# Turning v on VectorE instead of TensorE in a channel-attention and rational-FFN kernel, and adding sums of squares by accumulating DMA

## The chip, the core and the metric

The kernel runs on one core of a Trainium2 chip. The metric is the device time of one execution in microseconds (us): 2692.88 as the median of three runs, from 2692.05 to 2693.2. TensorE does the matrix products, VectorE, ScalarE and GpSimd the elementwise work, and SyncE issues the plain DMAs. In the rows these are PE (PEld is PE's weight load), DVE, ACT, POOL and SP.

## The reference

```python
# per batch b of 4: q, k, v are [6080, 256]
qn = q / (norm(q, axis=1) + 1e-6)        # norm of each column over the 6080 rows
kn = k / (norm(k, axis=1) + 1e-6)
s = kn.T @ qn / tau                      # [256, 256] for each batch
a = exp(s - s.max(-1)); a /= a.sum(-1) + 1e-9
x = (v @ a).reshape(24320, 256)
h = x @ w_in                             # [24320, 2048]
P = a0 + a1*h + a2*h**2 + a3*h**3
Q = 1 + |b0|*|h| + |b1|*h**2
out = (P / (Q + 1e-6)) @ w_out           # [24320, 256]
```

w_in and w_out are float64; everything else is float32.

## The kernel before, in words

The two products `v @ a` and `x @ w_in` are fused: for each batch the kernel forms `a @ w_in` once (`fuse`, eight pieces, split into a high and a low part `whi`, `wlo`), and then multiplies v by it. Precision is kept by such splits: v, too, is split into `vhi` and `vlo`.

Rows go in groups of 512 tokens (the last group of a batch has 448), 12 to a batch, 48 in all. For a group, `values` (line 740) loads v into `vst`, turns it so that its 256 columns lie on the partitions (eight TensorE transposes into a PSUM slot), copies the turned slot to `vhi` on ScalarE, and subtracts on VectorE to get `vlo`. Then eight calls of `pair` (line 766) each take 256 of the 2048 hidden columns: two times six matmuls give h in a PSUM slot `hx` (three slots of two banks), ScalarE, VectorE and GpSimd work out the rational function on tiles of 128x1024 or on halves of 128x512, and `mm2` multiplies by `w_out` into the PSUM tile `acc`. Four of the eight pairs (kind R) split their result into `gh` and `gl` for fast products; the other four (kind S) give one tile `g`, multiplied in full float32, for which the trace has two matmul records each. `finish` (line 884) copies `acc` to SBUF, turns it back on TensorE, copies it again and stores it.

Beside this runs the next batch's attention (`Attn.half`, line 538): 24 half tiles of k and q are loaded, multiplied (`products`), squared on ScalarE into one of two `sq` buffers, and added up on GpSimd into `ssq` for the norms. For batch 0 all of it stands before the first group, and its adds are shared by GpSimd and VectorE. Two batches take their 24 halves within some three groups shortly before they are needed; I call these groups those with score products, and the others, which do nothing but eight pairs and the two turnings, plain groups.

The order is found before anything is issued. Each piece of work is a `step` with an engine, a cost, a due time (`key`, from the tables LAG and TIME) and the buffers that it reads and writes. `Planner.order` runs these through a list scheduler: an engine that is free takes the ready step with the lowest key whose buffers fit the counts in SLOTS. The instructions are then issued in that order, and each engine runs its own in order, with semaphores between engines. So a wait on one instruction holds up everything behind it on that engine.

Of the kernel before, what the change touches and what calls it, by code (L numbers as in the profile page):

```python
# [20 lines left out]
LAG = {  # L21
    "first": (-23.943, 0.779, 16.152, -2.628, 12.275, -14.299, 0.849, 12.204),
    "second": (64.578, 55.323, 59.143, 56.607, 7.413, 49.338, 52.686, 69.362),
    "line": (11.809, -44.33, -0.798, -23.493, 7.232, -28.691, -20.654, -32.78),
    "prod": (-25.799, -25.066, -7.177, -0.027, 1.503, -30.754, -29.951, -14.021),
    "abs": (22.851, -16.828, -6.381, 4.349, 3.845, 0.375, -1.748, -5.521),
    "slope": (-2.413, -14.175, 23.292, -11.592, 10.064, 22.358, 14.327, 33.823),
    "num1": (102.929, 82.894, 81.158, 62.614, 64.142, 120.209, 89.073, 104.516),
    "num2": (-4.828, -66.826, -23.076, -34.364, -51.549, -56.374, -41.833, -65.959),
    "sum": (4.693, 16.192, 3.118, 9.167, 1.798, 5.734, -2.218, 21.491),  # L30
    "root": (8.815, 1.931, -7.534, -8.44, 11.521, 1.596, -18.294, 11.215),
    "one": (27.21, 31.412, 40.487, 22.316, 24.471, -12.593, 43.293, 5.876),
    "square": (-64.503, -49.599, -58.591, -28.542, -47.268, -42.996, -32.677, -8.585),
    "quot": (40.746, 32.008, 16.16, 51.527, 29.306, 35.7, 39.709, 24.527),
    "again": (-61.355, -87.995, -84.935, -58.616, -91.448, -79.4, -44.502, -69.519),
    "rest": (-17.013, -33.435, -9.224, -61.671, -10.183, -41.213, -23.935, -25.063),
    "last": (-39.442, -40.174, -68.15, -83.691, -21.902, -24.741, -46.676, -44.956),
    "last_pool": (-0.493, -59.623, -7.515, -32.037, 18.764, -45.886, -12.678, -10.454),
    "out": (63.96, 25.995, 31.164, 31.971, 24.821, 19.268, 27.921, 33.051),
    "out_lo": (116.352, 93.718, 68.074, 61.654, 91.315, 121.222, 76.822, 102.449),  # L40
}
TIME = {
    "pair": 6.5, "start": 92.588, "load": 1.191, "softmax": 58.031, "in": 2.437,
    "late_in": -22.444, "out0": -54.096, "out": 7.105, "attn0_0": 31.018, "attn_0": 1.206,
    "attn0": 69.854, "attn": 0.995, "attn1": 94.156, "value": 1.073, "fuse": 5.271,
    "finish": -40.738, "front": 35.456, "front_pace": 13.309, "back": 50.586, "store": 55.554,
    "ahead_pe": 283.994, "ahead_act": 1891641.487, "ahead_dve": 6393007968.0, "ahead_pool": 11581445.34,
# [3 lines left out]
KIND = ("RFP", "SU", "RFP", "SF", "RFP", "SU", "RFP", "SF")  # L51
# [59 lines left out]
def flat(bufs):  # L111
    return [x for b in bufs for x in (b.both if isinstance(b, Pair) else [b])]


class Planner:
# [5 lines left out]
    HOP = {"PE": 0.25, "ACT": 0.07, "DVE": 0.07, "POOL": 0.07, "SP": 3.5}  # L121
# [39 lines left out]
    def order(self):  # L161
# [113 lines left out]
def tile_channel_attention_rational_ffn(  # L275
# [41 lines left out]
    def apart(eng, ins):  # L317
# [15 lines left out]
    pool = InOrder(tc, nc.gpsimd, apart)  # L333
# [5 lines left out]
    plan = Planner(SLOTS, ("d", "uu", "r", "gh", "gl", "g", "w", "kq", "sq", "vst", "vhi", "vlo", "orow", "acc"), ("hA", "hB", "acc"),  # L339
# [176 lines left out]
    class Attn:  # L516
# [21 lines left out]
        def half(self, i, at, both, sps):  # L538
# [35 lines left out]
            else:  # L574
# [5 lines left out]
                step(*(("DVE", 1.2) if own else ("POOL", 2.38)), at + 2, fn, [sq, total], [total], True)  # L580
# [389 lines left out]
```

## Time and profile before

| what | us |
|---|---|
| median of three runs | 2692.88 |
| the profiled execution's own time | 2693.56 |
| its span, first to last instruction | 2691.8 |
| TensorE busy | 2601.5 (97%) |
| VectorE busy | 2473.1 (92%) |
| GpSimd busy | 2287.1 (85%) |
| ScalarE busy | 2238.9 (83%) |

The busy time of TensorE counts pipelined matmuls that overlap, so its real pace is read from the starts of neighbours in the timeline. The mean granted TensorE clock over the span is 0.992 of full speed. In the rows below, "x" is a count, and the number behind "|" is busy time in us and the mean of one in ns.

### The profile page before, as it was taken

How to read it: one execution, taken by the hardware profiler on the slowest of the kernel's cores; microseconds unless marked ns; L12 is line 12 of the kernel's file. 1: busy time of each engine (PE TensorE's matmuls, PEld its weight loads, DVE VectorE, ACT ScalarE, POOL GpSimd, SP SyncE). 2: the span in 40 equal slices, each digit the busy share in tenths (PEclk: the TensorE clock that was granted, in tenths of full speed). 3: DMA queues.
4: the chain of work that ended last, by engine and by line, in shares of the span. 5: the costliest groups of instructions: out<-in, count | busy, mean ns of one | idle time of the engine just before them, and what ended most of it. 6: DMA issues, size and time to landing. Idle time of an engine off the chain costs nothing.

```text
span 2691.8 us, 30390 instructions
## 1 busy us (share of the span) xinstructions
PE 2601.5 (97%) x10304; PEld 1864.0 (69%) x10304; DVE 2473.1 (92%) x2911; ACT 2238.9 (83%) x2285; POOL 2287.1 (85%) x1725
## 2 busy tenths in 40 slices
PE   7899999999999999999999999999999999999998
PEld 5766667666766666667777667667777666667666
DVE  8889998899979999998888999999888999999998
ACT  5688887788888888888878888888786888898896
POOL 6598888888768888889978898888996898898897
PEclk9899999999999999999999999999999999999999
DMA  9400002000100000012210000001220000000000
GB/s 318 139 18 16 24 16 85 16 16 31 41 22 16 24 24 16 24 40 77 79 60 15 32 15 17 32 16 47 78 77 24 23 8 24 32 8 24 31 9 15
DMA packets 69324, 109.97 MB, mean 41 GB/s; under 512 B 5296, under 2 KB 53936, under 8 KB 69168
## 3 DMA queue, kind: packets, MB, share of 16 engines
q1 hardware_dynamic: 69168, 108.03, 12.0%
q8 instruction: 81, 1.33, 0.2%
q14 instruction: 75, 0.61, 0.1%
HBM read 83.10 MB, written 24.90 MB: 40 GB/s over the span
## 4 chain that ended last, share of the span: by engine, by line
DVE 38%; PE 33%; POOL 11%; issue 8%; ACT 8%; DMA 1%; SPq 0%; DVEq 0%; POOLq 0%; ACTq 0%
PE hx L64 18%; PE acc L64 15%; DVE hx L64 13%; DVE d L64 9%; DVE uu L64 7%; POOL d L64 7%; DVE g L64 4%; DVE gh L64 3%; ACT uu L64 3%; ACT r L64 2%; POOL gl L64 2%; POOL ssq L64 2%; DVE vlo L64 1%; ACT d L64 1%; POOL orow L64 1%
## 5 line engine op out<-in xcount | busy, mean ns | idle before, releaser
L64 PE MATMUL hx<-vhi,w 128*128 128x512 f32 (+1 forms) x3072 | 1094.5, 413 | 42.4 <-DVE g L64 25.1
L64 PEld LDWEIGHTS hx<-vhi,w 128*128 128x128 f32 x3072 | 578.4, 188 | 240.2 <-DVE g L64 51.8
L64 PE MATMUL acc<-g,w_out_sb 128*128 128x512 f32 (+1 forms) x1536 | 688.9, 587 | 1.1 <-DVE g L64 1.1
L64 POOL TENSOR_TENSOR d<-d,gh 128x512 f32<-128x512 f32 (+1 forms) x384 | 484.2, 1282 | 192.4 <-DVE gh L64 191.9
L64 PE MATMUL hx<-vlo,w 128*128 128x512 f32 (+1 forms) x1536 | 598.5, 390 | 0.0
L64 ACT ACTIVATE uu<-hx,babs 128x1024 f32<-128x1024 f32 (+1 forms) x384 | 423.3, 1102 | 164.9 <-PE hx L64 163.1
L64 POOL TENSOR_TENSOR gl<-d,r 128x512 fp32r<-128x512 f32 (+1 forms) x384 | 489.7, 1283 | 19.9 <-DVE d L64 18.7
L64 DVE SCALAR_TENSOR_TENSOR hx<-uu,coef,hx 128x1024 f32<-128x1024 f32 (+1 forms) x384 | 488.9, 1273 | 3.5
L64 POOL TENSOR_TENSOR d<-d,r 128x512 f32<-128x512 f32 (+1 forms) x384 | 481.3, 1276 | 10.6 <-ACT r L64 8.1
L64 DVE TENSOR_TENSOR uu<-uu,hx 128x1024 f32<-128x1024 f32 (+1 forms) x384 | 461.7, 1202 | 27.8 <-ACT uu L64 27.0
L64 PEld LDWEIGHTS acc<-g,w_out_sb 128*128 128x128 f32 x1536 | 289.9, 189 | 273.1 <-issue 254.7
L64 ACT ACTIVATE uu<-hx,coef 128x1024 f32<-128x1024 f32 (+1 forms) x384 | 457.0, 1190 | 0.0
L64 ACT ACTIVATE r<-d 128x1024 f32<-128x1024 f32 (+1 forms) x384 | 401.9, 1047 | 37.6 <-POOL d L64 34.6
L64 ACT ACTIVATE d<-d 128x1024 f32<-128x1024 f32 (+1 forms) x288 | 301.4, 1047 | 140.7 <-DVE d L64 140.3
L64 ACT ACTIVATE r<-r 128x1024 f32<-128x1024 f32 (+1 forms) x384 | 402.2, 1048 | 5.7
L64 DVE SCALAR_TENSOR_TENSOR d<-uu,babs,hx 128x1024 f32<-128x1024 f32 (+1 forms) x288 | 364.2, 1264 | 29.3 <-ACT uu L64 25.9
L64 POOL TENSOR_SCALAR d<-d,ones 128x1024 f32<-128x1024 f32 (+1 forms) x288 | 322.6, 1120 | 78.0 <-ACT r L64 77.1
L64 PEld LDWEIGHTS hx<-vlo,w 128*128 128x128 f32 x1536 | 290.0, 189 | 72.6 <-issue 26.8
L64 DVE SCALAR_TENSOR_TENSOR d<-hx,coef,d 128x512 f32<-128x512 f32 (+1 forms) x384 | 282.9, 741 | 51.8 <-POOL d L64 51.6
L64 DVE SCALAR_TENSOR_TENSOR hx<-hx,coef,r 128x512 f32<-128x512 f32 (+1 forms) x384 | 288.4, 751 | 22.7 <-ACT r L64 13.4
L64 DVE SCALAR_TENSOR_TENSOR gh<-hx,coef,r 128x512 fp32r<-128x512 f32 (+1 forms) x384 | 269.4, 740 | 23.9 <-ACT r L64 15.4
L64 DVE SCALAR_TENSOR_TENSOR g<-d,hx 128x512 f32<-128x512 f32 (+1 forms) x384 | 257.3, 679 | 20.4 <-POOL d L64 6.5
(101 smaller groups left out, 2990.1 us busy)
## 6 DMA issues: line engine op xcount, KB each, us to landing
vst<-in_v_dram SPq DMA_DIRECT2D x44, 512.0 KB, 3.4
out_dram<-orow SPq DMA_DIRECT2D x44, 512.0 KB, 2.6
kq<-in_k_dram SPq DMA_DIRECT2D x78, 256.0 KB, 3.5
kq<-in_q_dram SPq DMA_DIRECT2D x78, 256.0 KB, 3.8
d<-in_moe_w_in_dram SPq DMA_DIRECT2D x8, 512.0 KB, 6.5
r<-in_k_dram SPq DMA_DIRECT2D x10, 256.0 KB, 6.0
r<-in_q_dram SPq DMA_DIRECT2D x10, 256.0 KB, 6.0
d<-in_moe_w_out_dram SPq DMA_DIRECT2D x4, 512.0 KB, 5.7
```

The lines of the kernel that those rows point to most:

```text
L64: ins = op(*args, **kwargs)
```

## The change

v is loaded in four DMAs that already place 32x32 blocks where they belong, in runs of 32 floats (128 bytes) instead of 4 KB, and one VectorE instruction turns the blocks. The turned v lies in one of the two `orow` buffers in SBUF, which `finish` uses as well, and no longer in a PSUM slot. GpSimd makes `vlo`. The sums of squares of batches 1 to 3 are added by a DMA issued from GpSimd that accumulates into `ssq`; each must wait until the one before has landed. Output rows are stored in four DMAs of 1 KB runs. The S pairs write their result over `y` instead of a buffer `g`, halves of `gh` and `gl` share a tile, there is one buffer less for the fused weights, the planner gets other delays between engines, and LAG and TIME have new numbers throughout. The kinds of pairs and their arithmetic are the same; `OUT` stays on TensorE.

```diff
 LAG = {
-    "again": (-61.355, -87.995, -84.935, -58.616, -91.448, -79.4, -44.502, -69.519),
+    "again": (-142.994, -152.496, -145.689, -152.346, -180.413, -123.122, -130.534, -108.094),
...
-KIND = ("RFP", "SU", "RFP", "SF", "RFP", "SU", "RFP", "SF")
+KIND = ("RFPh", "SUPh", "RFPh", "SFPh", "RFPh", "SUPh", "RFPh", "SFPh")
+OUT = "PE"
+SSQ = "DMA"
+VIN = "DVE"
+VLO = "POOL"
...
-    HOP = {"PE": 0.25, "ACT": 0.07, "DVE": 0.07, "POOL": 0.07, "SP": 3.5}
+    HOP = {"PE": 0.22, "ACT": 0.05, "DVE": 0.05, "POOL": 0.05, "SP": 3.5}
+    POOL_HOP = 0.09
+    SAME = {"PE": 0.0, "ACT": 0.03, "DVE": 0.1, "POOL": 0.05, "SP": 0.0}
...
-    SLOTS = {"hA": 3, "hB": 3, "acc": 1, "d": 3, "uu": 4, "r": 3, "gh": 6, "gl": 4, "g": 4, "w": 9, "kq": 4, "sq": 2, "ssq": 1,
+    SLOTS = {"hA": 3, "hB": 3, "acc": 1, "d": 3, "uu": 5, "r": 3, "gh": 3, "gl": 2, "w": 8, "kq": 4, "sq": 2, "ssq": 1,
...
                 fn = lambda: e.tensor_tensor(total[:pn], sq[:pn], total[:pn], op=ALU.add)
-                step(*(("DVE", 1.2) if own else ("POOL", 2.38)), at + 2, fn, [sq, total], [total], True)
+                if SSQ == "DMA" and not first:
+                    begun = Buf()
+                    fn = lambda: pool.dma_start(total[:pn], sq[:pn], accum_op=ALU.add)
+                    step("POOL", 1.0, at + 2, fn, [sq, total], [begun])
+                    step("SP", 0.1, at + 2, lambda: None, [begun, sq, total], [total])
+                else:
+                    step(*(("DVE", 1.2) if own else ("POOL", 2.38)), at + 2, fn, [sq, total], [total], True)
...
     def values(G, at, gate=()):
         vst = buf("vst", [P, T, C], F32)
-        slot = banks()
-        fn = lambda: sp.dma_start(vst[:pn], v[b, base : base + pn * T].rearrange("(p t) c -> p t c", t=T))
-        step("SP", 1.5, at - 3 * II, fn, gate, [vst])
-        def turned():
-            for c in range(NC2):
-                for t in range(T):
-                    pe.transpose(
-                        slot[:, c, t * pn : (t + 1) * pn], vst[:pn, t, c * P : (c + 1) * P], ident[:pn, :pn]
-                    )
-        step("PE", 1.1, at, turned, [vst], [slot, hi, lo])
-        step("ACT", 1.05, at + 1, lambda: act.activation(hi[:, :, :n], slot[:, :, :n], AF.Copy), [slot], [hi])
-        fn = lambda: dve.tensor_tensor(
-        step("DVE", 1.2, at + 2, fn, [slot, hi], [lo])
+        def load():
+                src = rows.rearrange("(j k) (e q i) -> q j k e i", k=K, q=4, i=32)
+                for x in range(4):
+                    dst = vst[32 * x : 32 * x + 32].rearrange("p t c -> p (t c)")[:, : K * 64]
+                    sp.dma_start(dst.rearrange("p (k e i) -> p k e i", e=NC2, i=32), src[x])
+        step("SP", 2.0, at - 3 * II, load, gate, [vst])
+            turned = buf("orow", [P, NC2, GT], F32, "vT")
+            def turn():
+                dve.transpose(
+                    turned[:, :, :n].rearrange("p e (k j) -> p k e j", j=32),
+                    vst.tile.rearrange("p t c -> p (t c)")[:, : K * 64].rearrange("p (k e i) -> p k e i", e=NC2, i=32),
+                )
+            step("DVE", 1.2, at, turn, [vst], [turned])
+        fn = lambda: act.activation(hi[:, :, :n], turned[:, :, :n], AF.Copy)
+        step("ACT", 1.05, at + 1, fn, [turned], [hi])
+        e, eng, cost = (dve, "DVE", 1.2) if VLO == "DVE" else (pool, "POOL", 2.38)
+        step(eng, cost, at + 2, fn, [turned, hi], [lo])
...
     def finish_pe(G, at, acc):
-        fn = lambda: sp.dma_start(out[row : row + pn * T].rearrange("(p t) e -> p t e", t=T), orow[:pn])
+        dst = out[row : row + n].rearrange("(i k) e -> i k e", k=K)
+        def send():
+            for x in range(4):
+                sp.dma_start(dst[:, x:K:4, :], orow[32 * x : 32 * x + 32, : len(range(x, K, 4))])
```

How the change moves instructions is seen in the order of each engine. First TensorE, near the end of a plain group of batch 1 (`ident` is the identity by which v, `vst`, is turned). Before:

```order
L64 MATMUL acc_92<-gl_146,w_out_hi 128x512 x2
L64 MATMUL acc_92<-g_149,w_out_sb 128x512 x2
L64 MATMUL acc_92<-g_150,w_out_sb 128x512 x2
L64 MATMUL hx_153<-ident,vst_130 128x128 x8
L64 MATMUL hx_151<-vhi_132,w_118 128x512
L64 MATMUL hx_151<-vlo_134,w_118 128x512
```

Now, at the end of the same group:

```order
L68 MATMUL hx_142<-vlo_134,w_121 128x512
L68 MATMUL hx_142<-vhi_132,w_129 128x512
L68 MATMUL acc_94<-gh_138,w_out_hi 128x512 x2
L68 MATMUL acc_94<-gh_138,w_out_lo 128x512 x2
L68 MATMUL hx_144<-vhi_131,w_114 128x512
L68 MATMUL hx_144<-vlo_133,w_114 128x512
```

The turning of v, which stood between the float32 products of one group and the next h in a PSUM slot of its own, is gone, and the next h follows other products.

Next VectorE in the same group, where the low part of v stood. Before:

```order
L64 SCALAR_TENSOR_TENSOR hx_152<-hx_152,coef,r_102 128x512 x2
L64 SCALAR_TENSOR_TENSOR g_147<-d_85,hx_152 128x512
L64 SCALAR_TENSOR_TENSOR g_148<-d_85,hx_152 128x512
L64 TENSOR_TENSOR uu_91<-uu_91,hx_153 128x1024
L64 TENSOR_TENSOR vlo_133<-hx_151,vhi_131 128x1024
L64 SCALAR_TENSOR_TENSOR hx_153<-uu_91,coef,hx_153 128x1024
L64 SCALAR_TENSOR_TENSOR gh_137<-hx_153,coef,r_101 128x512
L64 SCALAR_TENSOR_TENSOR gh_138<-hx_153,coef,r_101 128x512
```

Now:

```order
L68 SCALAR_TENSOR_TENSOR hx_142<-hx_142,coef,r_103 128x512 x2
L68 SCALAR_TENSOR_TENSOR uu_89<-d_87,hx_142 128x512
L68 SCALAR_TENSOR_TENSOR gh_137<-hx_144,coef,r_104 128x512
L68 SCALAR_TENSOR_TENSOR uu_89<-d_87,hx_142 128x512
L68 SCALAR_TENSOR_TENSOR gh_137<-hx_144,coef,r_104 128x512
L68 STREAM_TRANSPOSE orow_100<-vst_130 128x16x2x32
L68 SCALAR_TENSOR_TENSOR d_87<-uu_92,babs,hx_143 128x1024
```

`vlo` gives way to the turning of v; the halves of two pairs (`uu`, which takes the place of `g`, and `gh`) are now interleaved.

Then GpSimd in a group with score products of batch 1. Before:

```order
L64 TENSOR_TENSOR d_87<-d_87,r_103 128x512 x2
L64 TENSOR_TENSOR d_85<-d_85,gh_139 128x512
L64 TENSOR_TENSOR d_85<-d_85,gh_140 128x512
L64 TENSOR_TENSOR ssq_136<-sq_99,ssq_136 128x1024
L64 TENSOR_TENSOR gl_145<-d_85,r_102 128x512
L64 TENSOR_TENSOR gl_146<-d_85,r_102 128x512
L64 TENSOR_SCALAR d_86<-d_86,ones 128x1024
L64 TENSOR_TENSOR ssq_136<-sq_100,ssq_136 128x1024
L64 TENSOR_TENSOR d_86<-d_86,r_101 128x512 x2
```

Now:

```order
L68 TENSOR_TENSOR d_86<-d_86,gh_139 128x512 x2
L68 DMA ssq_136<-sq_102 128x1024
L68 TENSOR_TENSOR gl_141<-d_86,r_104 128x512 x2
L68 TENSOR_SCALAR d_87<-d_87,ones 128x1024
L68 DMA ssq_136<-sq_101 128x1024
L68 TENSOR_TENSOR d_87<-d_87,r_103 128x512 x2
L68 TENSOR_SCALAR d_88<-d_88,ones 128x1024
L68 TENSOR_SCALAR d_86<-d_86,babs 128x1024
L68 DMA ssq_136<-sq_102 128x1024
```

Each add of 128x1024 has become the issue of a DMA, with two or three other instructions between one and the next.

Last, GpSimd at the start, where batch 1's first accumulations stand ahead of the first group (the names in brackets are the semaphores waited for; DMASW0 to DMASW7 are those of the accumulating DMAs in turn):

```order
L68 DMA ssq_136<-sq_102 128x1024 [waits Activation_49]
L68 DMA ssq_136<-sq_101 128x1024 [waits DMASW0_49,Activation_49]
L68 TENSOR_TENSOR vlo_133<-orow_100,vhi_131 128x1024 [waits Activation_49]
L68 DMA ssq_136<-sq_102 128x1024 [waits DMASW1_49,Activation_49]
L68 DMA ssq_136<-sq_101 128x1024 [waits DMASW2_49,Activation_49]
L68 DMA ssq_136<-sq_102 128x1024 [waits DMASW3_49,Activation_49]
L68 DMA ssq_136<-sq_101 128x1024 [waits DMASW4_49,Activation_49]
```

Each accumulation waits for the one before; before the change these were adds, which follow each other on the engine.

## Rows read from the trace of the kernel before

**Rows 1.** The page's first part: busy time, share, instructions by engine.
```profile
PE 2601.5 (97%) x10304; PEld 1864.0 (69%) x10304; DVE 2473.1 (92%) x2911; ACT 2238.9 (83%) x2285; POOL 2287.1 (85%) x1725
```

**Rows 2.** Windows: length, busy us by engine, clock, DMA; plain groups, their sum.
```profile
2124.20:2627.70 503.50, 493.44 (x1921) 343.79 (x1921) 488.33 (x551) 437.16 (x431) 439.57 (x342) 1.00 0.06 20
sum 1511.00, PE 1480.65 PEld 1030.20 DVE 1464.27 ACT 1309.83 POOL 1318.58; mean PE 296.13 PEld 206.04 DVE 292.85 ACT 261.96 POOL 263.72
```

**Rows 3.** Timeline of TensorE: start us, length us, instruction, count.
```profile
1048.19 0.62 PE L64 MATMUL acc<-gh,w_out_hi 128*128 128x512 f32 x2
...
1049.56 3.59 PE L64 MATMUL acc<-g,w_out_sb 128*128 128x512 f32 x8
1052.99 1.04 PE L64 MATMUL hx<-ident,vst 128*128 128x128 f32 x8
1055.14 0.50 PE L64 MATMUL hx<-vhi,w 128*128 128x512 f32 x1 [1.12 <-DVE g L64]
```

**Rows 4.** Timeline of TensorE in a group with score products.
```profile
1310.21 1.04 PE L64 MATMUL acc<-ident,orow 128*128 128x128 f32 x8
1311.09 3.62 PE L64 MATMUL hx<-kq 128*128 128x256 f32 x16
```

**Rows 5.** Waits of TensorE in the plain groups from 1465 to 1818.5.
```profile
PE hx L64 <- DVE g L64: 5.2, 5, 1.2
```

**Rows 6.** Groups by form: count, busy us, mean ns, idle before it, releasers.
```profile
L64 DVE SCALAR_TENSOR_TENSOR hx<-uu,coef,hx 128x1024 f32<-128x1024 f32 x352 | 452.1, 1284 | 3.0
...
L64 DVE TENSOR_TENSOR uu<-uu,hx 128x1024 f32<-128x1024 f32 x352 | 427.1, 1213 | 14.5 <-ACT uu L64 13.7
...
L64 DVE SCALAR_TENSOR_TENSOR d<-uu,babs,hx 128x1024 f32<-128x1024 f32 x264 | 336.8, 1276 | 25.2 <-ACT uu L64 24.3 <-issue 0.8
...
L64 DVE SCALAR_TENSOR_TENSOR hx<-hx,coef,r 128x512 f32<-128x512 f32 x352 | 266.3, 757 | 21.4 <-ACT r L64 13.0 <-ACT uu L64 0.5
L64 DVE SCALAR_TENSOR_TENSOR d<-hx,coef,d 128x512 f32<-128x512 f32 x352 | 261.2, 747 | 46.6 <-POOL d L64 46.5
L64 DVE SCALAR_TENSOR_TENSOR gh<-hx,coef,r 128x512 fp32r<-128x512 f32 x352 | 248.6, 746 | 23.4 <-ACT r L64 15.4
...
L64 DVE SCALAR_TENSOR_TENSOR g<-d,hx 128x512 f32<-128x512 f32 x352 | 238.0, 684 | 17.6 <-POOL d L64 4.6 <-DVE hx L64 0.5
...
L64 POOL TENSOR_TENSOR d<-d,uu 128x1024 f32<-128x1024 f32 x88 | 211.7, 2406 | 3.4 <-ACT uu L64 0.5
L64 POOL TENSOR_TENSOR ssq<-sq,ssq 128x1024 f32<-128x1024 f32 x63 | 151.6, 2407 | 35.6 <-ACT sq L64 28.9 <-DVE w L64 6.4
...
L64 DVE TENSOR_TENSOR vlo<-hx,vhi 128x1024 fp32r<-128x1024 f32 x44 | 53.6, 1218 | 3.9 <-ACT vhi L64 3.9
```

**Rows 7.** Timeline of VectorE, three neighbours and what follows them.
```profile
1037.89 0.75 DVE L64 SCALAR_TENSOR_TENSOR d<-hx,coef,d 128x512 f32<-128x512 f32 x1
1038.55 1.21 DVE L64 TENSOR_TENSOR uu<-uu,hx 128x1024 f32<-128x1024 f32 x1
1039.80 1.29 DVE L64 SCALAR_TENSOR_TENSOR hx<-uu,coef,hx 128x1024 f32<-128x1024 f32 x1
1041.19 1.55 DVE L64 SCALAR_TENSOR_TENSOR hx<-hx,coef,r 128x512 f32<-128x512 f32 x2
```

**Rows 8.** Windows: a group with score products; the time before the first group.
```profile
0.00:101.00 101.00, 78.29 (x313) 63.86 (x313) 83.62 (x133) 55.42 (x74) 54.45 (x30) 0.90 0.75 254
1276.70:1340.00 63.30, 62.74 (x258) 46.69 (x257) 52.76 (x61) 51.27 (x52) 63.05 (x45) 1.00 0.27 84
```

**Rows 9.** DMA issues of the page: KB each, median us to landing.
```profile
vst<-in_v_dram SPq DMA_DIRECT2D x44, 512.0 KB, 3.4
...
d<-in_moe_w_in_dram SPq DMA_DIRECT2D x8, 512.0 KB, 6.5
```

**Rows 10.** Timeline of the start, GpSimd and ScalarE.
```profile
66.05 2.35 POOL L64 TENSOR_TENSOR ssq<-sq,ssq 128x1024 f32<-128x1024 f32 x1 [4.82 <-ACT sq L64]
...
104.15 1.11 ACT L64 ACTIVATE uu<-hx,babs 128x1024 f32<-128x1024 f32 x1 [1.41 <-PE hx L64]
```

More of the change, by code (lines that the diff above doesn't have):

```diff
@@ L36 @@
[L36 to L40, printed above, removed]
+    "first": (28.264, 1.351, 30.596, -31.998, 48.265, -7.633, 5.766, 9.407),
@@ L44 @@
[L44 to L47, printed above, removed]
-}
-KIND = ("RFP", "SU", "RFP", "SF", "RFP", "SU", "RFP", "SF")
+    "pair": 6.5, "start": 100.961, "load": 1.875, "softmax": 71.531, "in": 4.844,
@@ L382, in run @@
                 b.tile = b.view(b.slot)
-            used = {(b.slot, b.tag == "hB") for b in own.values()}
-            half[0] = used.pop() if len(used) == 1 and (eng == "PE" or lone) else None
+            at = {(b.slot, b.tag == "hB") for b in own}
+            if len(at) == 1:
+                half[0] = *at.pop(), {(b.tag, b.slot) if b.tag else id(b) for b in rest}
             fn()
@@ L411, in tile_channel_attention_rational_ffn @@
     for kind in KIND:
-        W_AT.append(count[kind[0]])
-        count[kind[0]] += 2
+        W_AT.append(count["S" if kind[0] == "S" else "R"])
+        count["S" if kind[0] == "S" else "R"] += 2
     w_out_sb = const.tile([P, count["S"], C], F32, name="w_out_sb") if count["S"] else None
@@ L790, in pair @@
         for i in range(2):
[L791 to L799 removed]
+            step("PE", 1.39 * s, at + 0.01 * i, lambda i=i: mm1(i), [whi, wlo, vhi, vlo], [hx.both[i]])
@@ L801, in cost, with mm2, put @@
+        def mm2(w, x, parts, first, last):
+            for i in parts:
+                for a, g in zip(w, x):
+                    for e in range(NC2):
+                        pe.matmul(
+                            acc[:, e, :n], a[:, W_AT[p] + i, e * P : (e + 1) * P], g[:, i, :n],
+                            start=(first and i == parts[0] and a is w[0]), stop=(last and i == 1 and a is w[-1]),
+                        )
         def cost(per, fixed):
             return per * s + fixed
-        if kind[1] == "F":
+        def put(eng, per, fixed, name, fn, reads, writes, rank=None, port=False, later=0.0):
+            key = at + LAG[name][p] + later
+            step(eng, cost(per, fixed), key, fn, reads, writes, port, None if rank is None else at + rank)
@@ new lines, in pair, with part @@
+        put("ACT", 0.87, 0.2, "square", fn, [r], [r])
+        old = [acc] if p else []
+        end = p == NFP - 1
+        halves = [[0], [1]] if kind[3] == "h" else [[0, 1]]
+        if kind[0] in "RQ":
+            ghi, glo = buf("gh", [P, 2, GT], F32R), buf("gl", [P, 2, GT], F32R)
+            ghi_ok, glo_ok = ([Buf() for _ in halves] for _ in range(2))
+        t_ok, e_ok = ([Buf() for _ in halves] for _ in range(2))
+        def part(b, k):
+            return b[:, k[0] : k[-1] + 1, :n]
```

284 lines of the change are left out of this document (191 added, 93 removed).

## The prediction

> **What bounds the kernel now.** I read the busy shares first, then windows over stretches without score products, then the timelines of TensorE and VectorE inside one plain group, and last the start. The shares say little: four engines lie between 83 and 97% [rows 1]. The windows say where time can be won. Five stretches hold 30 plain groups in 1511.00 us, 50.37 each, and the longest gives 50.35; both TensorE and VectorE are busy for 97 to 98% of them, GpSimd for 87%, at full clock [rows 2]. So a plain group has two candidates, and I work out a floor for each from single durations.
>
> TensorE: a group has 144 matmuls of 512 columns at full pace, four S pairs and two turnings. Six matmuls take 1049.56 − 1048.19 = 1.37 us if I count from their start to the S pair's, 0.228 each; the S pair's eight records take 1052.99 − 1049.56 = 3.43 [rows 3]; a turning, from its start to the next, 0.88 [rows 4]. That is 32.9 + 13.7 + 1.8 = 48.4. (The first of these rows covers two of the six; the other four stand in the left-out lines between.)
>
> VectorE: 8 × (1.284 + 1.213) + 6 × 1.276 + 8 × (0.757 + 0.747 + 0.746 + 0.684) + 1.218 = 52.3 us of 55 instructions [rows 6]. Neighbours on different tiles overlap: the next starts 0.085 before the last has ended, so 55 × 0.085 = 4.7 comes off, 47.6. A follower that reads what its forerunner wrote doesn't overlap: `hx` after `uu` starts 0.04 late and a half after the whole `hx` 0.10 late [rows 7], thus 0.12 and 0.2 worse than an unrelated one. VectorE's whole order has 196 followers of the first kind and 223 of the second, 196 × 0.12 + 223 × 0.2 = 68 us, 1.4 per group. Floor: 49.0, which the measured 48.8 of busy time [rows 2] bears out.
>
> The remaining 1.35 us of a plain group is waiting that the two engines hand each other: with only three `hx` slots, and v's turning taking one of them for as long as ScalarE and VectorE read it, TensorE waits at `hx` for VectorE's last reader, 5.2 us over seven groups, 0.74 per group [rows 5], and 1.12 at one place right behind the turning [rows 3]. The other 18 groups are different: a group with score products has TensorE busy 62.74 and GpSimd 63.05 of 63.30 us, VectorE only 52.76 [rows 8]. Before the first group 101 us pass [rows 8].
>
> **The change, part by part.**
>
> *v's turning leaves TensorE.* 48 times 0.88 us go, and the slot stays free for h. TensorE's floor falls to 47.5.
>
> *VectorE gets the turning and gives up `vlo`.* The turning has no row. It is one pass over 128x1024 with one input in SBUF; the nearest row is VectorE's `vlo` on the same shape, 1218 ns, and I take 1.2. Below, a half of that shape costs 684 to 757 ns, and as it is a pass over twice as much I go no lower than 0.8; above, I take GpSimd's 2406 ns for two inputs of the shape [rows 6]. At 1.2 the exchange is even. The halves of two pairs are now interleaved, so that fewer stand behind their own forerunner: 153 followers at 0.2 and 222 at 0.12, 57 us, 1.2 per group. VectorE's floor: 48.8. The turning waits for v's four loads and for an `orow` buffer; behind it stand the next pairs' halves, so if it waits, VectorE does. The single `vst` is refilled as soon as it has been turned, a whole group ahead: even four loads and four stores one after the other at 3.4 us each [rows 9] are 27 us of 49. I cost this wait at nothing; if the cover were gone, each us would cost 48.
>
> *`vlo` on GpSimd* takes 2.4 by the same row. GpSimd's 43.96 per plain group [rows 2] becomes 46.4 of about 49, still below the other two, though close. ScalarE's `vhi` reads SBUF instead of PSUM; ScalarE has 43.7 of 50.35 [rows 2], so a small difference either way is covered.
>
> *Plain groups.* Both floors fall, TensorE's by more, so VectorE alone binds. Of the 50.37 I take off the 0.23 that the followers save and the 0.74 of slot waits: 49.4, which leaves VectorE 0.6 idle. 30 × 0.97 = **29 us won**.
>
> *The other 18 groups* are TensorE's, so they win the turning, 18 × 0.88 = 16. GpSimd, which was as full there, loses an add of 2.4 for each half tile and gets an issue instead. No row shows one: between nothing and the add itself, I take 1.0, as the sequencer has little to compute; 69 × 1.4 = 97 us less work, of which I count 2 us, since TensorE stays. **18 us won.**
>
> *The accumulating DMAs.* Each waits for the one before, and the wait stands in GpSimd's own queue: everything behind it, the `d` and `gl` of the pairs above all, waits with it, and then VectorE and TensorE. What decides is T, from issue to landing. No row shows an accumulation. Below stands v's load of the same 512 KB at 3.4 us; above, twice the 6.5 us of the loads in the busy start [rows 9], as the target is read too: 13. Three transfers of 512 KB where the load has two make 3.4 × 1.5 = 5.1; I take 5.5. In batches 2 and 3, 23 accumulations fall in about three groups, 3 × 63.3 = 190 us, 8.3 apart. GpSimd's other work there, 63.05 × 3 − 23 × 2.4 = 134, with 23 issues 157, spreads to 6.8 between two. At 5.5 the wait is hidden.
>
> By the Trainium skill ("DMA: Bandwidth & Descriptors", Anatomy of one DMA — SWDGE (gpsimd) path) a transfer issued from GpSimd takes about 2.0 us and then its bytes at 436 GB/s; an estimate by that page is 3.2 us for 512 KB, with which the start below would cost nothing, and 2646 would come out. No run here shows it yet for an accumulation.
>
> *The start.* Batch 1's first accumulations now stand ahead of the first group. The first add begins at 66.05 [rows 10], and with two `sq` buffers ScalarE's work for the first pair stands behind the square that needs the seventh accumulation landed: 66.05 + 7 × 5.5 = 104.5, and 1 for the square, 105.5, where the first pair's operation began at 104.15 [rows 10]. I book **2 us lost** (none at 3.4; 8.4 at 6.5; 54 at 13).
>
> In that stretch the DMA engines are busy for 75% [rows 8]. v's pieces of 128 bytes fall on it; the Trainium skill (the same page, Specifications) wants pieces of at least 512 bytes for the full rate, and if the first load thus landed some 24 us later than at 3.4, the start would lose up to 10 us and the time would be 2656. In plain groups, with DMA at 6% [rows 2], the rule has 49 us of cover.
>
> **Sum.** −29 − 18 + 2 = −45 from the profiled execution's 2693.56 (its span of 2691.8 and 1.8 around it; 0.7 above the median), so 2648.
>
> **The rivals.**
>
> *More is won.* With the slot free VectorE may lose its 0.6 of idle, and half of the followers' cost as well: 48.2. For it: TensorE at 47.5 would allow it. Against: three `hx` slots remain for eight pairs, and before the change the two never came nearer than 1.35. 30 × 2.17 + 18 = 83, 2610.
>
> *The turning eats the gain.* If it costs 2.3, VectorE's floor is 49.9 and plain groups stay at 50.4. For it: VectorE is as full as TensorE, and nothing is taken from it. Against: one input, not two. Only the 18 groups win, 16: 2678. The same holds if GpSimd at 46.4 holds the pairs back.
>
> *Slower: the chain of accumulations.* If T passes 8.3 us, 23 of them outlast the stretch of batches 2 and 3; GpSimd stands at each, and the start grows by 7 T. Loss: 2 × 23 × (T − 8.3) + 7 T − 38 = 53 T − 420, against 47 won; from T = 8.8 on the kernel is slower than before. At 9.75, midway between 6.5 and 13, it loses 97: 2744. For it: read, add and write through a chain that admits one at a time. Against: DMA is at 27% in such a group [rows 8], so nothing crowds it.
>
> **Chances.** Forecast 0.56, own range 2630 to 2670 (start 0 to 10, plain groups 48.9 to 49.9); more won 0.14; turning eats it 0.15; chain of accumulations 0.15. A difference under 0.2%, some 5 us, can't be told from none. Of the third case 0.03 and of the last 0.03 end there, 0.01 of the first; slower keeps 0.12; faster has the rest, 0.81. The range 2606 to 2692 leaves out the better part of the last case and a little below.
>
> **What would show it.** The profile after should have STREAM_TRANSPOSE near 1.2 us and `vlo` on GpSimd near 2.4; windows of plain groups at 49.4 with VectorE at 98 to 99% and TensorE below it; TensorE's wait at `hx` for VectorE per group less than 0.74; the accumulations landing in 4 to 7 us, with GpSimd's waits for DMA a few us in all; the first pair's operation at 104 to 108. The forecast is wrong if plain groups stay above 50 us, if a wait for v's loads appears at the turning, or if GpSimd waits at accumulations for longer than its neighbours can spare.

## The result, and the profile after

The changed kernel takes 2664.27 us (median of four runs, 2655.84 to 2666.34); the kernel before took 2692.82 beside it. The ratio is 0.9888, 95% interval 0.9867 to 0.9910: 28.5 us or 1.1% faster. The forecast was 2648. The profiled execution has a span of 2664.3 us, 27.5 less than before. First its busy shares:

```profile
PE 2555.0 (96%) x9920; PEld 1829.5 (69%) x9920; DVE 2463.1 (92%) x2911; ACT 2235.7 (84%) x2287; POOL 2301.2 (86%) x1773
```

Against [rows 1] they barely move, so the place of the gain has to come from windows. Here are 31 plain groups (2 to 10, 16 to 19, 25 to 32 and 37 to 46) in four stretches, with the sum (length, busy us by engine, clock, DMA share):

```profile
232.10:673.90 441.80, 433.84 (x1657) 302.63 (x1656) 432.22 (x491) 387.66 (x382) 412.10 (x313) 1.00 0.12 22
...
2103.40:2594.90 491.50, 481.74 (x1842) 336.35 (x1841) 482.67 (x549) 437.21 (x431) 461.26 (x350) 1.00 0.10 20
sum 1524.00, PE 1494.03 PEld 1042.57 DVE 1495.57 ACT 1348.87 POOL 1427.59; mean PE 373.51 PEld 260.64 DVE 373.89 ACT 337.22 POOL 356.90
```

A plain group takes 1524.00 / 31 = 49.16 us, where it took 50.37 [rows 2]. Groups 13 to 15 and 20, which hold no score products either, aren't among them; group 13 took 54.1, and with these four the mean is 49.30. The very 30 groups of [rows 2] went from 1511.0 to 1478.8 us. VectorE is busy for 98% of the 1524 us and GpSimd for 94% (87% before). The prices of the new operations, by form, and the landing of the accumulations, from the page:

```profile
L68 DVE STREAM_TRANSPOSE orow<-vst 128x1024 f32<-128x1024 f32 x44 | 54.4, 1235 | 7.0 <-DMA vst<-in_v_dram 6.8 <-issue 0.3
L68 POOL TENSOR_TENSOR vlo<-orow,vhi 128x1024 fp32r<-128x1024 f32 x44 | 106.3, 2417 | 7.6 <-ACT vhi L68 7.6
L68 POOL DMA_DIRECT2D ssq<-sq x69 | 63.2, 916 | 80.3 <-DMA ssq<-sq 49.8 <-ACT sq L68 10.3 <-ACT kq L68 8.6
...
ssq<-sq POOLq DMA_DIRECT2D x63, 512.0 KB, 5.7
```

1.235, 2.417, 0.92 and 5.7 us stand against 1.2, 2.4, 1.0 and 5.5 in the forecast. But the third row also says that GpSimd stood idle for 49.8 us at accumulations.

Where the time went, by stretch (read from the start of each group's first product):

| stretch | before | after | difference |
|---|---|---|---|
| start to the end of group 10 | 682.5 | 673.9 | -8.6 |
| groups 11, 12 (into batch 1) | 124.4 | 124.4 | 0.0 |
| 13 to 20 | 405.5 | 398.6 | -6.9 |
| 21 to 24 (score products, into batch 2) | 252.6 | 256.4 | +3.8 |
| 25 to 32 | 406.6 | 393.7 | -12.9 |
| 33 to 36 (score products, into batch 3) | 252.6 | 256.4 | +3.8 |
| 37 to 46 | 503.5 | 491.5 | -12.0 |
| 47 | 64.1 | 69.4 | +5.3 |

From group 25 on the plain stretches win more than was forecast. The groups with score products, which should have won, don't. Part of their +3.8 is a matter of place: before, 16 of a batch's 192 score matmuls stood in groups 20 and 32 already, and none do now. From 20 to 24 it is 305.6 us before and 305.9 after, and from 32 to 36 305.7 in both. Windows of the time before the first group and of groups 22, 23, 34 and 35 (the clock is the third column from the end, then the DMA share and GB/s):

```profile
0.00:107.90 107.90, 81.59 (x336) 67.00 (x337) 74.52 (x123) 55.50 (x71) 50.50 (x32) 0.93 1.02 281
...
1258.50:1327.70 69.20, 66.07 (x265) 48.56 (x264) 58.71 (x67) 57.71 (x57) 58.75 (x48) 1.00 0.74 169
1327.70:1399.40 71.70, 66.25 (x280) 52.19 (x278) 59.97 (x84) 53.79 (x65) 52.90 (x47) 0.95 0.43 91
1908.60:1979.70 71.10, 67.46 (x265) 49.74 (x264) 59.08 (x68) 57.80 (x58) 59.43 (x48) 0.98 0.74 165
1979.70:2049.50 69.80, 64.50 (x279) 51.30 (x278) 60.17 (x85) 50.52 (x61) 52.34 (x46) 0.98 0.33 62
```

The start has the DMA engines busy throughout (1.02, where it was 0.75). The landing of the accumulations in a window from 50 to 110 us, and ScalarE behind the seventh of them:

```profile
ssq<-sq POOLq DMA_DIRECT2D x7, 512.0 KB, 7.9
```

```profile
116.33 1.06 ACT L68 ACTIVATE sq<-kq 128x1024 f32<-128x1024 f32 x1 [1.94 <-DMA ssq<-sq]
117.29 1.10 ACT L68 ACTIVATE uu<-hx,babs 128x1024 f32<-128x1024 f32 x1
```

The first pair's operation (the second of these lines) began at 104.15 before [rows 10] and begins at 117.29 now, right behind a square that waited for an accumulation.

GpSimd, at 63.05 of 63.30 us before [rows 8], has room now, and yet groups 22 and 34 take 69.2 and 71.1 us, where they took 63.3. Some 3.6 us of this are 16 score matmuls more than they held before, at the price of [rows 4]. Waits in group 34, in us, times and longest:

```profile
ACT sq L68 <- DMA ssq<-sq: 9.0, 6, 3.2
POOL ssq L68 <- DMA ssq<-sq: 7.3, 5, 2.0
```

Both are waits for accumulations. Groups 22 and 34 each hold 11 of a batch's 23: 69.2 / 11 = 6.3 and 71.1 / 11 = 6.5 us from one to the next, little more than the landing of 5.7, which is counted from the issue.

### The profile page after: what moved, and what is told of

The parts are those of the page before. It is cut to its first block, busy times and chain, and to the rows that moved or that the text cites. A ratio compares the mean times of both kernels' runs of the same rounds, so it can differ in the third digit from the quotient of the medians.

```text
span 2664.3 us, 30195 instructions
## 1 busy us (share of the span) xinstructions
PE 2555.0 (96%) x9920; PEld 1829.5 (69%) x9920; DVE 2463.1 (92%) x2911; ACT 2235.7 (84%) x2287; POOL 2301.2 (86%) x1773
## 4 chain that ended last, share of the span: by engine, by line
PE 44%; DVE 27%; ACT 8%; DMA 8%; issue 7%; POOL 5%; SPq 0%; DVEq 0%; POOLq 0%; ACTq 0%
PE hx L68 24%; PE acc L68 20%; DVE d L68 9%; DVE hx L68 8%; DVE uu L68 6%; DMA ssq<-sq 5%; ACT uu L68 4%; POOL d L68 4%; DVE gh L68 2%; ACT r L68 2%; DMA kq<-in_q_dram 2%; DVE orow L68 1%; ACT d L68 1%; POOL gl L68 1%; DMA r<-in_q_dram 1%
## 5 line engine op out<-in xcount | busy, mean ns | idle before, releaser
L68 PE MATMUL hx<-vhi,w 128*128 128x512 f32 (+1 forms) x3072 | 1109.2, 415 | 54.4 <-DVE d L68 37.9
L68 PE MATMUL acc<-uu,w_out_sb 128*128 128x512 f32 (+1 forms) x1536 | 690.8, 589 | 1.9 <-DVE uu L68 1.9
L68 POOL TENSOR_TENSOR gl<-d,r 128x512 fp32r<-128x512 f32 (+1 forms) x384 | 497.8, 1312 | 65.5 <-DVE d L68 23.7
L68 POOL TENSOR_TENSOR d<-d,r 128x512 f32<-128x512 f32 (+1 forms) x384 | 488.2, 1301 | 31.1 <-ACT r L68 30.2
L68 PEld LDWEIGHTS acc<-uu,w_out_sb 128*128 128x128 f32 x1536 | 291.2, 190 | 278.9 <-issue 259.3
L68 POOL TENSOR_SCALAR d<-d,ones 128x1024 f32<-128x1024 f32 (+1 forms) x288 | 326.2, 1135 | 49.5 <-ACT r L68 49.2
L68 DVE SCALAR_TENSOR_TENSOR uu<-d,hx 128x512 f32<-128x512 f32 (+2 forms) x392 | 261.5, 677 | 20.7 <-POOL d L68 9.2
```

The costliest lines, as they stand in the source:

```text
L68: ins = op(*args, **kwargs)
```

## The experiments

My theory at first: VectorE sets the plain groups; accumulations and v's small pieces keep the rest from winning. Rivals: the order of the work alone, or a GpSimd that is too full.

**e1, v turned twice.**

```diff
-                dve.transpose(
+                for _ in range(2):
+                    dve.transpose(
```

> The changed kernel with v turned twice by VectorE (the second turn writes the same values again); the order of all other instructions is the same. If VectorE binds the plain groups, as the forecast has it, each of them grows by a whole turn, 1.15 to 1.24 us, from 49.2 to about 50.4, and the time rises by 35 to 50 us to about 2705. The rival, that TensorE or the round trips between engines set the pace and VectorE is only full, lets a plain group grow by less than 0.4 and the time by less than 15.

2716.31 us, ratio to before 1.0088 (1.0074 to 1.0102). Groups 37 to 46:

```profile
2140.90:2644.10 503.20, 484.79 (x1842) 335.73 (x1841) 493.99 (x558) 438.22 (x431) 461.78 (x350) 1.00 0.10 19
```

503.20 against 491.50: 1.17 per group; from group 38 to 45 a group took 50.5 instead of 49.2, no less than a whole turn. VectorE binds the plain groups now. The total rose by 52, slightly more than I expected.

**e2, the adds back on GpSimd.**

```diff
-SSQ = "DMA"
+SSQ = "POOL"
```

> The changed kernel with the sums of squares of batches 1 to 3 added by GpSimd again, the order found anew. If the accumulating DMAs are what costs the groups with score products their gain (GpSimd and ScalarE waiting for one accumulation after the other), the four groups from 21 to 24 fall from 256.4 us to 252 or less, the start shortens by 5 to 8 us, and the time is 2640 to 2655. The rival is that GpSimd, which also has v's low part now, has no room for the adds: then the four groups take more than 260 us and the time is 2670 or more. Plain groups stay at 49.2 in both.

2732.32 us, 1.0145 (1.0132 to 1.0159). Groups 21 to 24:

```profile
1227.70:1501.60 273.90, 251.84 (x1018) 190.69 (x1016) 216.15 (x270) 208.62 (x227) 237.96 (x167) 0.97 0.23 61
```

273.9 us against 256.4, the end of group 1 at 254.6 against 232.1, plain groups at 49.2. The rival holds: with `vlo` on GpSimd the adds no longer fit, and the accumulating DMAs save 68 us against this version. Part of the 68 may belong to an order that its offsets were not made for; that was not tried.

**e3, v of groups 0 and 1 by TensorE.**

```diff
+        vin = "PE" if G < 2 else VIN
...
-            if VIN == "DVE":
+            if vin == "DVE":
...
-        e, eng, cost = (dve, "DVE", 1.2) if VLO == "DVE" else (pool, "POOL", 2.38)
+        e, eng, cost = (dve, "DVE", 1.2) if VLO == "DVE" or vin == "PE" else (pool, "POOL", 2.38)
```

> The changed kernel with v of groups 0 and 1 alone loaded in 1 KB runs, turned by TensorE, with its low part made by VectorE; everything else as changed. If the loads of v in 128-byte pieces cost the start (they hold SyncE's queue for 8 us each there, and VectorE stands 6.4 us at the turning of group 1), the time from 0 to the end of group 1, 232.1 us, falls by 6 to 12 and the total to about 2655. The rival, that the accumulations behind batch 1's squares set the start, leaves it within 2 us.

2690.86 us, 0.9994 (0.9985 to 1.0003); the end of group 1 came at 243.6. Neither theory expected that: the scheduler made another order of the start. It says nothing on the pieces, only that an experiment that changes the order mixes two things. From e5 on the order stays as it was.

**e4, the offsets alone.**

```diff
-SSQ = "DMA"
-VIN = "DVE"
-VLO = "POOL"
+SSQ = "POOL"
+VIN = "PE"
+VLO = "DVE"
```

> The changed kernel with v loaded in 1 KB runs and turned by TensorE into a PSUM slot, its low part on VectorE and the sums of squares added by GpSimd: what is left of the change are the new offsets, delays and tiles. If the turning and its slot are what shortened the plain groups, they are back at 50.2 to 50.8 us and the time is 2685 to 2705. The rival, that the new order of VectorE's halves made the gain, leaves them at 49.2 to 49.6.

2816.65 us, 1.0461 (1.0446 to 1.0475). Groups 37 to 46:

```profile
2209.50:2741.90 532.40, 499.25 (x1916) 340.89 (x1914) 487.97 (x551) 435.65 (x431) 438.06 (x341) 1.00 0.07 19
```

53.2 us per plain group: worse than either kernel. The new offsets win nothing without the new ways of turning v, making `vlo` and adding the squares. How much of the gain each gives where they are together can't be read from this.

**e5, v in whole runs.**

```diff
-                src = rows.rearrange("(j k) (e q i) -> q j k e i", k=K, q=4, i=32)
+                src = rows.rearrange("a c -> (a c)").rearrange("(q j f) -> q j f", q=4, j=32)
...
-                    sp.dma_start(dst.rearrange("p (k e i) -> p k e i", e=NC2, i=32), src[x])
+                    sp.dma_start(dst, src[x])
```

> The changed kernel in the same order of instructions, with v's four loads of a group taking the same bytes in whole runs (3.5 to 4 KB for each partition) instead of pieces of 128 bytes; the rows so land in the wrong place, and the output is not the reference's. If the pieces cost the start (each load holds SyncE's queue for 8 us there), the time to the end of group 1 falls from 232.1 us by 6 to 10, and the total by as much. The rival, that the accumulations and the order set the start, leaves it within 2 us. Plain groups stay at 49.2 in both.

2663.26 us, 0.9891 (0.9878 to 0.9905); first product at 108.0, end of group 1 at 230.8. SyncE's first v load, of the changed kernel and of this one:

```profile
56.97 8.13 SPq L68 DMA_DIRECT2D vst<-in_v_dram  x4
```

```profile
57.26 2.60 SPq L68 DMA_DIRECT2D vst<-in_v_dram  x4
```

The queue is held 5.5 us less, and nothing comes of it. By the rule that full rate wants pieces of 512 bytes (the Trainium skill, "DMA: Bandwidth & Descriptors", Specifications) I had put up to 10 us on the pieces. They cost nothing that can be told from scatter: the first product came at 105.4 and the end of group 1 at 229.3 in e12, where the start is that of the changed kernel.

**e6, short accumulations.**

```diff
-                    fn = lambda: pool.dma_start(total[:pn], sq[:pn], accum_op=ALU.add)
+                    fn = lambda: pool.dma_start(total[:pn, :128], sq[:pn, :128], accum_op=ALU.add)
```

> The changed kernel in the same order, with each accumulating DMA adding only an eighth of the columns of the squares (64 KB; the norms are then wrong). It keeps the issue on GpSimd and the chain, and takes away most of the 5.7 us of landing. If waiting for the landing is what costs the groups with score products, the four groups from 21 to 24 fall from 256.4 us by 4 to 6, those from 33 to 36 as well, and the start by 3 to 8: in all 12 to 20 us. If the order of the work sets them, all three fall by less than 2.

2628.28 us, 0.9757 (0.9744 to 0.9770): 36 us less than the changed kernel. Landing, the start, groups 22 and 23:

```profile
ssq<-sq POOLq DMA_DIRECT2D x63, 64.0 KB, 3.3
...
0.00:98.10 98.10, 78.66 (x336) 65.16 (x337) 75.54 (x123) 57.16 (x75) 51.41 (x33) 0.97 0.97 284
1242.50:1307.80 65.30, 65.08 (x266) 48.88 (x265) 58.09 (x67) 57.55 (x57) 57.94 (x48) 1.00 0.45 108
1307.80:1372.10 64.30, 62.49 (x279) 50.00 (x277) 56.70 (x83) 52.89 (x64) 52.11 (x46) 1.00 0.26 61
```

Of the 38.9 us between the two profiled executions, 15.7 come by the end of group 1 and 11.3 each in groups 21 to 24 and 33 to 36; groups 21 and 33, with five accumulations each, stay at 61.6 us. It takes away wait and bytes at once, which e9 and e10 part. Group 23's 7.4 puzzled me, since GpSimd waits little there; e12 came of it.

**e7, e8 and e11: the kernel before with less to do.** e7 turns only one block of eight of v on TensorE, e8 makes an eighth of its low part on VectorE, e11 both. The edit of e11 (m is 64 from group 2 on):

```diff
-                for t in range(T):
+                for t in range(T if G < 2 else 1 - c):
...
-            lo[:, :, :n], slot[:, :, :n], hi[:, :, :n].bitcast(F32), op=ALU.subtract
+            lo[:, :, :m], slot[:, :, :m], hi[:, :, :m].bitcast(F32), op=ALU.mult if G > 1 else ALU.subtract
```

> The kernel before in the same order, with seven of the eight TensorE transposes of v left out from group 2 on, the copy to the high part scaled and the low part a product so that the numbers stay finite (the output is meaningless). TensorE has 0.77 us less to do in a group, while the slot is held as before. If TensorE alone bound the plain groups before, they fall from 50.37 by 0.7 to 0.8; if VectorE is tied with it, as the forecast has it, by 0.2 to 0.5; if VectorE alone bound them, by less than 0.1.

> The kernel before in the same order, with VectorE making only 64 of the 512 columns of v's low part from group 2 on (the rest of the buffer keeps old values): VectorE has about 1.0 us less to do in a group. If VectorE bound the plain groups alone, they fall from 50.37 by 0.9 to 1.0; if it was tied with TensorE, by 0.2 to 0.5; if TensorE bound them, by less than 0.1.

> The kernel before in the same order, with both left out from group 2 on: seven of the eight transposes of v on TensorE and 448 of the 512 columns of its low part on VectorE (the output is meaningless). If the two engines were tied, a plain group falls by 0.7 to 1.1 us from 50.25, where either alone gave 0.1 or nothing. The rival is that the slot of v, still held here, is what costs: then it falls by less than 0.3, or rises as with the transposes alone.

Ratios to before 1.0063 (1.0050 to 1.0077), 0.9982 (0.9972 to 0.9991) and 1.0038 (1.0023 to 1.0053). The last ten plain groups took 50.97, 50.26 and 50.72 us, where before had 50.35. With the transposes left out TensorE is done earlier and waits longer for the same slot, and every second group becomes slower. One such place of e7, in TensorE's timeline, and windows over it:

```profile
2330.92 0.27 PE L64 MATMUL hx<-ident,vst 128*128 128x128 f32 x1
2333.06 0.50 PE L64 MATMUL hx<-vhi,w 128*128 128x512 f32 x1 [1.87 <-DVE g L64]
```

```profile
2333.00:2334.00 1.00, 0.94 (x4) 0.81 (x5) 1.00 (x3) 0.37 (x1) 1.00 (x2) 1.00 0.89 352
2334.00:2335.00 1.00, 1.00 (x5) 0.76 (x4) 1.00 (x2) 0.00 (x0) 0.33 (x1) 0.54 0.00 0
2335.00:2336.00 1.00, 1.00 (x4) 0.81 (x3) 1.00 (x2) 0.00 (x0) 0.00 (x0) 0.50 0.00 0
2336.00:2337.00 1.00, 1.00 (x3) 0.79 (x3) 1.00 (x1) 0.00 (x0) 0.00 (x0) 0.50 0.00 0
2337.00:2338.00 1.00, 1.00 (x5) 0.74 (x4) 0.96 (x3) 0.29 (x1) 0.00 (x0) 0.75 0.00 0
```

After the wait the granted clock falls from 2.4 to 1.2 GHz for some 3 us; after the 1.12 us of [rows 3] it did not. None of the three expectations that a relieved engine shortens the group came true. In e7 the groups between the slower ones, 49.5 us where before had 49.6, hardly fall either. So the floor of neither engine alone held a plain group before. What is left is the hand-over at the slot, as e11's rival has it; no run frees the slot by itself, so this is argued and not shown.

**e9 and e10, two totals, and a third buffer.** Even and odd accumulations go to two totals (the first odd one is a plain copy), and VectorE adds the second in at the end; e10 adds a buffer for the squares.

```diff
+                        to = odd if i % 2 else total
+                        if i == 1:
+                            pool.dma_start(to[:pn], sq[:pn])
+                        else:
+                            pool.dma_start(to[:pn], sq[:pn], accum_op=ALU.add)
...
+                    for x in (odd[:, : 2 * C], odd[:, 2 * C :]):
+                        dve.tensor_tensor(total[:, : 2 * C], total[:, : 2 * C], x, op=ALU.add)
```

```diff
+                if not first:
+                    sq.view = lambda slot: (homes["sq"] + [sq2])[i % 3]
```

> The changed kernel in the same order, with whole accumulations that go by turns into two totals, so that each waits only for the one before the last; a second total of 4 KB for each partition is added, and VectorE adds the two at the end of a batch (1.4 us). If it is the wait for the one before that costs the 36 us which the short accumulations gave back, about half or more returns: GpSimd's waits for accumulations fall from 49.8 to under 20 us and the time to 2630 to 2648. The rival is that the short ones helped by moving less data, or by freeing ScalarE's two buffers of squares, which wait for the landing as before: then less than 8 us return.

> The kernel with two totals and a third buffer for the squares, again in the same order. If ScalarE's wait for a free buffer of squares is the second half of the cost, the groups from 21 to 24 and from 33 to 36 come down to the 245 us that they took with short accumulations, the start to about 98 us, and the time to 2626 to 2638. The rival, that the amount of data counts, leaves it within 4 us of the kernel with two totals alone.

e9 2666.84 us, 0.9902 (0.9888 to 0.9917); e10 2660.30, 0.9886 (0.9869 to 0.9902). GpSimd's waits for accumulations are gone in both, and the time hardly moved: my theory that the wait for the one before costs the 36 us falls. By place, group 22 took 67.6 and 66.7 us (69.2 changed, 65.2 short), group 34 68.7 and 66.6 (71.1, 65.2). In group 34 the waits are most of the cost, some 4.5 us; in group 22 they are 1 to 2.5, as e5 and e12, with whole accumulations in one chain, had 67.7 and 68.7 there. At the start the first pair's operation came at 113.8 in e10, against 117.3 changed, 114.6 in e5 and 104.6 with short accumulations: there the waits are a small part. Against that, the final adds in e9, timeline of VectorE:

```profile
231.94 1.74 DVE L68 TENSOR_TENSOR ssq<-ssq 128x512 f32<-128x512 f32 x1
233.71 3.32 DVE L68 TENSOR_TENSOR ssq<-ssq,ssq_odd 128x512 f32<-128x512 f32 x2
```

Each of the three takes some 1.7 us, where an addition of this shape takes 0.69 when undisturbed, and group 2 grew from 48.3 to 53.9 us. Without these 5.5 us e10 would have given back some 9.5 of the 36, still less than a half.

**e12, small sums in PSUM.** What disturbs them shows in group 23 of the changed kernel: VectorE, then GpSimd, then TensorE.

```profile
1366.49 0.74 DVE L68 TENSOR_TENSOR y<-n,s 128x4 f32<-128x4 f32 x1
1367.26 1.07 DVE L68 TENSOR_TENSOR e<-y 128x4 f32<-128x4 f32 x1
1368.37 0.94 DVE L68 TENSOR_TENSOR e<-n,e 128x4 f32<-128x4 f32 x1
1369.35 0.16 DVE L68 SCALAR_TENSOR_TENSOR e<-e,s 128x4 f32<-128x4 f32 x1
1369.54 1.94 DVE L68 SCALAR_TENSOR_TENSOR e<-y,e 128x4 f32<-128x4 f32 x1
```

```profile
1366.05 2.26 POOL L68 TENSOR_TENSOR d<-d,gh 128x448 f32<-128x448 f32 x2 [0.89 <-DVE n L68]
1368.29 1.01 POOL L68 TENSOR_SCALAR d<-d,babs 128x896 f32<-128x896 f32 x1
1369.39 2.07 POOL L68 TENSOR_TENSOR d<-d,uu 128x896 f32<-128x896 f32 x1
```

```profile
1372.59 0.74 PE L68 MATMUL hx<-vhi,w 128*128 128x448 f32 x1 [4.34 <-DVE d L68]
```

Four columns of work take up to 1.94 us, and the three longest end within some 20 ns of a GpSimd instruction's end (1368.31, 1369.30, 1371.46); the one that began in GpSimd's gap, from 1369.30 to 1369.39, took 0.16. VectorE's `d` stands behind them, and TensorE waits 4.34 us for it. In the kernel before, these sums waited too, here with their shortest, median and longest in ns, but TensorE had other work beside those of group 23, from 1393.07 to 1395.92:

```profile
L64 DVE TENSOR_TENSOR e<-y x4: 162/1012/1075, 69.7 to 2052.8; 128x4 f32<-128x4 f32 x4
L64 DVE TENSOR_TENSOR e<-n,e x4: 161/552/946, 69.9 to 2053.9; 128x4 f32<-128x4 f32 x4
```

```profile
1394.53 3.17 PE L64 MATMUL acc<-g,w_out_sb 128*128 128x448 f32 x8
```

So it is the new order that makes them costly. In e6 two of the four long ones took 0.16 us each, so its group 23 came down in part by this, and not by a shorter wait for a landing.

```diff
-                dve.tensor_tensor(y.tile, n2.tile, s0.tile, op=ALU.mult)
-                dve.tensor_tensor(e.tile, y.tile, y.tile, op=ALU.mult)
-                dve.tensor_tensor(e.tile, n2.tile, e.tile, op=ALU.subtract)
...
+                dve.tensor_tensor(y.tile, scr(0), s0.tile, op=ALU.mult)
+                dve.tensor_tensor(scr(1), scr(0), s0.tile, op=ALU.mult)
+                dve.tensor_tensor(e.tile, scr(1), y.tile, op=ALU.mult)
+                dve.tensor_tensor(scr(2), scr(0), e.tile, op=ALU.subtract)
```

`scr` is a piece of the PSUM slot that holds the norms; two more instructions are changed in the same way.

> The changed kernel with the small sums of the norms (128x4, seven VectorE instructions in a batch) kept in PSUM wherever both inputs lay in SBUF, so that each reads at most one input from SBUF; one instruction of this size more, the order otherwise the same. If these instructions, which take 0.74 to 1.94 us and end when a GpSimd instruction ends, wait because both engines read SBUF through the same way, they fall to about 0.16 us each, TensorE's wait of 4.34 us in the groups 23 and 35 goes, with the slower clock behind it, each of these groups falls from 71.7 and 69.8 us to about 64 to 66, and the time to 2645 to 2656. The rival, that small instructions behind one another are slow for another reason, leaves them at 0.5 us or more and the time within 3 us of 2664.

2652.75 us, 0.9856 (0.9839 to 0.9873). The same sums, one by form, and groups 23 and 35:

```profile
L68 DVE SCALAR_TENSOR_TENSOR e<-hx,e 128x4 f32<-128x4 f32 x4 | 0.6, 162 | 0.1
...
1324.60:1390.10 65.50, 63.41 (x278) 49.77 (x277) 56.41 (x85) 53.87 (x65) 53.06 (x47) 1.00 0.48 99
1971.20:2035.90 64.70, 62.59 (x280) 49.99 (x278) 56.56 (x86) 49.93 (x61) 52.20 (x45) 1.00 0.37 68
```

All of them take 0.15 to 0.17 us, the groups lose 6.2 and 5.1 us, and the clock stays at 1.00. (Group 35 took 67.0 to 72.2 us in e5, e9 and e10, where the sums are as in the changed kernel, so its 5.1 is the less certain.) Of the versions that leave nothing out this is the fastest. The Trainium skill has the rule ("SBUF — State Buffer", Who interferes with whom): a VectorE instruction with two inputs in SBUF contends with a GpSimd instruction that reads SBUF, and one with at most one such input, outside VectorE's modes that use both ports, does not. The trace agrees, 0.74 to 1.94 against 0.16 us, and I had not weighed it.

## Why the prediction was right, and where it was wrong

*Plain groups: right.* Forecast 49.4, measured 49.16; the same 30 groups won 32.2 us, where I had 29. That VectorE binds is shown by e1; that it binds alone is not, since no run shortens TensorE's part now. The split was wrong: I let the slot waits go, yet TensorE still waits at `hx` for VectorE, 9.0 us in nine groups, 1.0 per group where I had asked for less than 0.74:

```profile
PE hx L68 <- DVE d L68: 7.6, 9, 0.8
PE hx L68 <- DVE uu L68: 1.4, 7, 0.2
```

What fell is VectorE's busy time per group, 48.83 to 48.27, and its idle time, 1.5 to 0.9. And the reading of before as two tied floors was not borne out by e7, e8 and e11.

*The other 18 groups: the step that failed.* "18 us won" there, less 2 at the start, should have been 16; the profiled executions lost 4.7 outside the 30 plain groups (27.5 − 32.2). TensorE did lose its 0.88 us in each, but waits took the place. By stretch, with the forecast's own terms, groups 20 to 24 and 32 to 36 should have won 8.8 us together and lost 0.3, groups 11 and 12 should have won 1.8 and won nothing, and the last should have won 0.9 and lost 5.3; the 2 us that I booked for GpSimd are missing as well. Up to group 10 the terms give 8.2, and 8.6 were won, but e6 shows that 15.7 more were to be had there. So the total lies in the range partly by luck: plain groups, and GpSimd's relief below, cover for costs that I had at 2 us or at nothing. Three costs are in it, partly hidden by a gain.
- "At 5.5 the wait is hidden" failed through the spacing, not through the landing: I spread 23 accumulations evenly, 8.3 apart, but 11 stand in one group, 6.3 to 6.5 apart. e6 gives back 4.0 and 6.0 us in groups 22 and 34, and e10 more than half of that.
- At the start I priced seven landings in a row at 5.5 us and booked 2 us. The order of things was as I had it, but the landings took 7.9, and the first pair's operation came at 117.29, not at 104 to 108; the first product came 6.9 later, at 107.9 (105.1 to 108.0 in e1, e5 and e12). The wait for the one before is a small part: in e10, without it, the first pair's operation still came at 113.8. By GB/s times length, 254 × 101 us = 25.7 MB were moved before the first group, then 30.3, and 27.9 in e6. The 2.4 MB between the last two, at some 283 GB/s, are about 8.6 us of the 9.8 that e6 gave back. So it fits that batch 1's earlier transfers, the accumulations among them, make the start bound by bytes, which also lengthens each landing. That it is bytes and not pieces fits e5; that the other 2.2 MB of 30.3 over 25.7 matter in the same way is worked out, not tried.
- The small sums at the batches' ends, in no term of mine, cost 6.2 and 5.1 us (e12), about half of it as a slower clock.
- Against these, GpSimd's relief, which I booked at 2 us, seems to be larger: with waits and bytes taken away (e6) the kernel is well below the forecast, at 2628, and groups 20 to 24 take 294.7 us, 10.9 less than before, of which the turning explains 4.4. No run measures the relief by itself.

*The other signs.* GpSimd's waits for accumulations were to be a few us in all and were 49.8. The wait for v's loads at the turning, a sign that the forecast is wrong, did appear, 6.8 us in all, but 6.4 of it at one turning before the first product and none that holds the plain groups; e5, which shortens the issue of these loads, won nothing.

*The last group,* 5.3 us longer, I had not foreseen at all. TensorE waits there 1.39 and 1.80 us for GpSimd's `gl`; why the new order ends worse was not tried.

*The rivals.* More won and the turning at 2.3 did not come; the chain that makes it slower asked for a landing above 8.3, and it was 5.7. By the estimate of 3.2 us for 512 KB from the Trainium skill's formula ("DMA: Bandwidth & Descriptors", Anatomy of one DMA — SWDGE (gpsimd) path) the start would have cost nothing; accumulations landed in 5.7, and in 7.9 at the start, so my 5.5 was nearer.

## What to carry to other kernels

Count a chain of waits by the densest group, not by its mean over a stretch: the 5.7 us of landing cost nothing where five stood in a group of 61.6 us, and some us where eleven did. To learn whether an engine binds, double one of its instructions in an unchanged order; leaving work out or switching a part back under a scheduler changes the order or the clock with it. A small VectorE instruction with both inputs in SBUF can last until the GpSimd instruction beside it ends (up to 1.94 us here, against 0.16), so keep one input in PSUM where it stands in front of something that others wait for.

## What the runs showed of the hardware that I had not expected

TensorE's clock fell to 1.2 GHz after a single wait: 1.87 us in e7, and 4.34 us in the changed kernel, which was then at half clock for 6 us, so that some 3 us of work were added to the wait. Windows over it:

```profile
1372.50:1373.50 1.00, 0.91 (x2) 0.83 (x3) 1.00 (x5) 0.00 (x0) 0.00 (x0) 0.50 0.00 0
...
1377.50:1378.50 1.00, 1.00 (x5) 0.87 (x4) 1.00 (x2) 0.17 (x1) 0.00 (x0) 0.50 1.02 158
1378.50:1380.00 1.50, 1.50 (x9) 1.37 (x8) 1.43 (x3) 1.50 (x2) 0.00 (x0) 0.99 0.94 168
```

An accumulating DMA of 512 KB landed in 5.7 us and one of 64 KB in 3.3: an estimate from the two is 2.9 us and then some 190 GB/s. In the start, with the DMA engines busy throughout (1.02), the larger ones took 7.9. The executions of the changed kernel lie 10.5 us apart, those of before 1.2 beside them and 4.6 at most in the later rounds; why was not tried.
